# A global filter and a GELU layer on one core: half of one batch's input behind the batch before's read-back, table parts at other slots, and another spacing of the last batch

## The chip, the core and the metric

The kernel runs on one core of a Trainium2 chip. A core has a matrix engine (TensorE, PE in the profile; PEld is its loading of weights), three engines for vectors and scalars (VectorE or DVE, ScalarE or ACT, GpSimd or POOL), an engine that here only issues transfers (SyncE or SP), and 16 DMA engines that all transfers share. Each engine works through its own list of instructions in order and waits for the others by semaphores. The metric is the device time of one execution in microseconds (us); lower is better.

## What is computed

The input `x` has 8 batches of 3008 rows by 256 channels. The first half filters every channel of a batch along the rows by a product of Fourier transforms; the second half is a layer with exact GELU over all 24064 rows, with 2048 hidden columns:

```python
X = np.fft.rfft(x, axis=1)
Y = X * (filt_r + 1j * filt_i)[None, :, :]
y = np.fft.irfft(Y, n=3008, axis=1)            # 8 x 3008 x 256
h = y.reshape(24064, 256) @ w_in               # 256 x 2048
g = 0.5 * h * (1.0 + erf(h / sqrt(2)))
out = g @ w_out                                # 2048 x 256
```

## The kernel before

**The layer** runs over 47 tiles of 512 rows. A tile needs 16 calls of `mm1` (one 128-column piece of the hidden layer each: two matmuls into a bank of PSUM, then GELU on ScalarE into `g_sb`, L643). The second product (`mm2_seven`, L700) uses Strassen's scheme: seven products of quarters in place of eight. For it VectorE forms sums of quarters of `g_sb` (`sums_1`, L685; `sums_2`, L691; `sums_3`, L698), and combines the products in `t_sb` and `ost` (L731 to L745). `put_rows` stores finished rows from GpSimd's queue (L763). The buffers of `t_sb` and `ost` rotate through four places, three of which a tile uses, so tile 4's second `ost` (written from L739 on) reuses the place of tile 3's first, which is stored last of tile 3's.

**The filter** writes 3008 as 47 x 64 and does four small transforms per batch, with two trips through HBM to turn the data round:

- `load_next` (L148): GpSimd waits at a *gate*, a copy of one element of a given tile (`gate`, L143), and then issues the loads of a quarter of the next batch's input (`load_x_pairs`; two DMAs for half `h` = 0, four for `h` = 1). Four pieces `c`, two halves each. Both batches use one buffer.
- `fold` (L102) on VectorE, then `s1` (L415): matmuls, evacuation to `a_sb` by ScalarE and VectorE (L326, L328), written to an HBM scratch R1 from SyncE's queue.
- `r1` (L442) reads R1 into `b_sb`. For each of three units `u`: `s2` (L448) multiplies by a table, `s2_out` multiplies by the filter on VectorE (L468, four calls), `s2_sum` adds (L474, L475), `s3` (L477) transforms back, `s3_out` evacuates to `v_sb` on ScalarE and writes a scratch R2 (L498). The `s2` of the next unit uses the same four banks that the `s3` before it used.
- `r2` (L501) reads R2 back into `d_sb` (L506), in four pieces. `s4` (L509) makes 16 half units of a batch with the table `T4a` and evacuates them to `y_sb`, the input of `mm1`, on ScalarE (L326) or VectorE (L330).

Batch 0 goes through a form of its own ahead of the layer. The rest is interleaved with it.

**Order.** The order is written out by hand. A *slot* is one call of `mm1` (16 to a tile, 752 in all); `put(slot, f, ...)` hangs a call onto a slot, and what is emitted in a slot stands in each engine's list ahead of that slot's share of `mm2_seven` and its `mm1`. A slot number therefore sets an order and not a time. Tile 5 is special (`late`): it needs the first unit of batch 1, so slots 80 to 85 hold a double share of the second product and no `mm1`, and `s4` of batch 1's first two units stands at slots 82 to 85. `first(b)` is the first slot of the tile in which batch `b` begins; `s1`, `s2` and `s3` of a batch are set back from it by fixed numbers. A set of `busy` slots, made from these, moves the `s4` units to free slots, and `crowd` says which of them go to ScalarE.

**Tables.** `T4a`, the table of `s4`, is made on GpSimd in four parts of eight columns (`table_4_all`, L403): each part has four multiplies (L411) and two sums (L413). Units 2i and 2i + 1 of a batch read part i. Its scratch tile comes from the same three buffers as `d_sb`.

Of the kernel before, what the change touches and what calls it, by code (L numbers as in the profile page):

```python
# [31 lines left out]
class _Mix:  # L32
# [114 lines left out]

    def load_next(self, b, p, c, h):  # L148

        self.gate(self.st[b, "p", p][0:1, p % 2, 1, 0, 0:1])  # L150
        self.load_x_pairs(b + 1, c, h)

    def load_w_in(self):
# [631 lines left out]
def kernel(  # L785
# [9 lines left out]
    m = _Mix(ctx, tc, x, filt_r, filt_i, moe_w_in, moe_w_out, out)  # L795
    nc, B, S = tc.nc, m.B, m.S
# [116 lines left out]
    def put(slot, f, *a):  # L913
        at.setdefault(slot, []).append((f, a))

    def first(b):
        return (b * S // TCH) * 16

    busy, crowd, after = set(), set(), {}
    for b in range(1, B):  # L920
        hi = first(b)
        e = 4 * (b == B - 1)
        s1, n1, r1 = (4, 2.75, 16) if b == 1 else (hi - 87, 3.7, hi - 73) if b == 2 else (hi - 94 - e, 3.7, hi - 80 - e)
        s2 = (30, 43, 56) if b == 1 else (hi - 64 - 2 * e + (b == 2), hi - 48 - 3 * e + e // 4, hi - 32 - 3 * e)
        busy.update(range(s1 - 1, s1 + int(3 * n1) + 2))
        for c in range(4):
            slot = s1 + int(c * n1 + (b == 1 and c in (1, 2)))
            put((0, 1, 5, 8)[c] if b == 1 else (70, 74, 86, 94)[c] if b == 2 else hi - 94 - (20, 13, 8, 6)[c], m.fold, b, c)
            put(slot, m.s1, b, c)
        for u in range(3):  # L930
            put(r1 if u < 2 else s2[0] + 1, m.r1, b, u)
            put(s2[u], m.s2, b, u)
            for i in range(4):
                put(s2[u] + 2 * i + (b == 2 and u == 0), m.s2_out, b, u, i // 2, i % 2)
            for i in range(2):
                put(s2[u] + (9 + i if 1 < b < B - 1 else 7 + 2 * i), m.s2_sum, b, 2 * u + i)
            s3 = s2[u] + (13 if 1 < b < B - 1 else 11)
            put(s3, m.s3, b, u)
            put(s3 + 1, m.s3_out, b, u, 1)
            busy.update(range(s2[u] - 1, s2[u] + 5), range(s3 - 1, s3 + 2))  # L940
        after[b] = s3 + 4
        crowd.update(range(s2[0], after[b]), range(s1 + 66, s1 + 94))
        if b + 1 < B:
            for i, (u, o, p) in enumerate(((0, 5, 1), (0, 7, 1), (1, 1, 2), (1, 5, 3), (1, 7, 3), (2, 1, 4), (2, 5, 5), (2, 7, 5))):
                put(s2[u] + o, m.load_next, b, p, i // 2, i % 2)

    for b in range(1, B):
        end = 1000000
# [26 lines left out]
    put(14, m.table_4_factors, g)  # L975
    put(18, m.table_u)
    parts = [(w, h) for w in range(0, HB, 8) for h in range(2)]
    for i, slot in enumerate((15, 22, 45, 52)):
        put(slot, m.table_4_all, parts[2 * i:2 * i + 2])
    put(1, m.load_filters_again, nc.gpsimd, 0, 2)  # L980
    put(18, m.load_filters_again, nc.sync, 2, 4)
# [57 lines left out]
```

## Time and profile before

| | |
|---|---|
| median of 3 runs | 741.06 us (741.05 to 741.15) |
| the profiled execution | 740.78 us, span of the core 739.0 us |
| granted TensorE clock | 0.999 |
| busy: PE, DVE, ACT, POOL | 97%, 82%, 78%, 39% of the span |
| moved by DMA | 89.30 MB, mean 121 GB/s |

The span runs from the first to the last instruction. A row of the timeline gives start, length, engine, line, operation, output and inputs; in square brackets stands the time for which the engine had been idle and what ended that. "x7" is a row that merges seven like instructions. A row of the chain gives start, length and what the chain passed through. A row of the waits gives the total, how often, and the longest. Lengths of matmuls are modelled. Slots fall at these times: slot 22 ends at 56.7, slot 45 at 80.0, slot 52 at 86.0, slot 71 at 104.5, slot 79 at 110.9, slot 104 at 136.9 and slot 582 at 580.1 on TensorE; other engines may run ahead or behind.

### The profile page before, as it was taken

Reading aid. Unit: us, or ns where it says so; the run is one execution under the profiler, and the core shown is the slowest. Engines: PE = TensorE matmul, PEld = TensorE weight load, DVE = VectorE, ACT = ScalarE, POOL = GpSimd, SP = SyncE. Lnnn points to the kernel's source line nnn. Section 1 sums busy time; section 2 is a strip of 40 time slices with the busy share of each in tenths; the row PEclk is TensorE's granted clock in tenths of the full one; section 3 lists DMA queues with packets and bytes.
Section 4 is the critical chain, followed back from the end, with each engine's and each line's share of the span. In section 5 each row is a group of like instructions: output and inputs, shape, how many; then the busy total and the mean of one; then the engine's idle time right before and its main releaser. Section 6 shows DMA issues by size and latency. Waiting matters only on the chain.

```text
span 739.0 us, 22144 instructions
## 1 busy us (share of the span) xinstructions
PE 716.6 (97%) x9063; PEld 506.7 (69%) x9213; DVE 604.0 (82%) x1105; ACT 575.6 (78%) x1049; POOL 290.8 (39%) x547
## 2 busy tenths in 40 slices
PE   7998999999999999999999999999999999999998
PEld 4855665667777767676777667666667667777776
DVE  8987797899887998788986999779988898676566
ACT  6996677778887888778887788877888777777773
POOL 7898771346122653134611364115631122122121
PEclk9999999999999999999999999999999999999999
DMA  9996443755345643545535455345544433401011
GB/s 150 211 192 201 105 112 94 209 128 109 85 129 173 124 99 106 155 138 115 124 116 172 105 123 126 101 150 146 113 101 137 137 99 96 115 31 58 30 58 59
DMA packets 81190, 89.30 MB, mean 121 GB/s; under 512 B 13201, under 2 KB 60433, under 8 KB 81089
## 3 DMA queue, kind: packets, MB, share of 16 engines
q0 software_dynamic: 22480, 40.02, 23.5%
q1 hardware_dynamic: 58193, 47.66, 23.3%
q8 instruction: 72, 1.18, 0.7%
q14 instruction: 29, 0.24, 0.1%
q10 hardware_dynamic: 416, 0.20, 0.1%
HBM read 55.57 MB, written 48.23 MB: 140 GB/s over the span
## 4 chain that ended last, share of the span: by engine, by line
PE 87%; ACT 4%; DVE 3%; DMA 3%; issue 2%; POOL 0%; SPq 0%; another core or an unknown queue 0%; DVEq 0%; POOLq 0%; ACTq 0%
PE ps_o L716 38%; PE ps_h L640 37%; PE ps_s L515 3%; PE ps_s L430 2%; PE ps_o L656 2%; ACT g_sb L643 2%; PE ps_s L457 2%; PE ps_s L488 2%; DMA R<-v_sb 1%; ACT v_sb L326 1%; DVE p L468 1%; DMA d_sb<-R 1%; DMA x_sb<-in_x_dram 1%; PE ps_c L587 1%; ACT y_sb L326 1%
## 5 line engine op out<-in xcount | busy, mean ns | idle before, releaser
L643 ACT ACTIVATE g_sb<-ps_h 128x512 f16<-128x512 f32 x752 | 445.8, 603 | 141.1 <-PE ps_h L640 116.5
L640 PE MATMUL ps_h<-y_sb,w_in_sb 128*128 128x512 bf16 (+3 forms) x1454 | 414.4, 365 | 0.6
L763 POOL DMA_DIRECT2D out_dram<-ost x231 | 131.2, 575 | 398.5 <-DVE ost L745 390.0
L716 PEld LDWEIGHTS <-g_sb 128*128 128x128 f16 x2880 | 189.0, 98 | 84.5 <-issue 13.5
L716 PEld LDWEIGHTS <-s_sb 128*128 128x128 f16 x2160 | 145.0, 98 | 53.6 <-issue 3.7
L640 PEld LDWEIGHTS <-w_in_sb 128*128 128x128 bf16 x1600 | 125.7, 98 | 7.7 <-issue 1.3
L716 PE MATMUL ps_o<-w_sums,g_sb 128*128 128x128 f16 x1440 | 124.8, 220 | 2.4 <-DVE g_sb L691 1.0
L716 PE MATMUL ps_o<-w_sums,s_sb 128*128 128x128 f16 x1440 | 123.4, 219 | 1.7 <-DVE t_sb L731 0.2
L685 DVE TENSOR_TENSOR s_sb<-g_sb 128x1024 f16<-128x1024 f16 x180 | 119.5, 696 | 0.7 <-ACT g_sb L643 0.6
L716 PE MATMUL ps_o<-w_out_sb,g_sb 128*128 128x128 f16 x1440 | 116.5, 220 | 2.5 <-DVE ost L745 0.7
L468 DVE TENSOR_TENSOR p<-ps_s,F 128x1024 bf16<-128x1024 f32 x84 | 102.0, 1218 | 7.8 <-PE ps_s L457 6.2
L99 POOL DMA_DIRECT2D x_sb<-in_x_dram x156 | 79.0, 513 | 2.5 <-DMA x_sb<-in_x_dram 1.4
L716 PE MATMUL ps_o<-w_out_sb,s_sb 128*128 128x128 f16 x720 | 62.5, 219 | 0.9
L691 DVE TENSOR_TENSOR g_sb<-s_sb,g_sb 128x1024 f16<-128x1024 f16 x90 | 62.1, 691 | 1.5
L698 DVE TENSOR_TENSOR s_sb<-g_sb 128x1024 f16<-128x1024 f16 x90 | 61.5, 683 | 0.0
L738 DVE TENSOR_TENSOR t_sb<-t_sb,ps_o 128x256 f32<-128x256 f32 x45 | 18.8, 419 | 41.6 <-PE ps_o L716 41.1
L515 PEld LDWEIGHTS <-d_sb 96*128 96x128 bf16 x448 | 31.2, 97 | 28.6 <-DMA d_sb<-R 2.8
L326 ACT ACTIVATE y_sb<-ps_s 128x376 bf16<-128x376 f32 x95 | 45.5, 479 | 4.6 <-PE ps_s L515 4.6
L326 ACT ACTIVATE v_sb<-ps_s 128x512 bf16<-128x512 f32 x83 | 45.6, 610 | 1.6 <-PE ps_s L488 1.3
L745 DVE TENSOR_TENSOR ost<-t_sb,ps_o 128x256 f32<-128x256 f32 x88 | 32.9, 416 | 15.6 <-PE ps_o L716 15.6
L328 DVE CAST a_sb<-ps_s 128x512 bf16<-128x512 f32 x54 | 34.7, 684 | 11.6 <-PE ps_s L430 11.4
L733 DVE TENSOR_TENSOR ost<-t_sb,ps_o 128x256 f32<-128x256 f32 x45 | 18.7, 416 | 27.6 <-PE ps_o L716 27.6
(156 smaller groups left out, 565.4 us busy)
## 6 DMA issues: line engine op xcount, KB each, us to landing
out_dram<-ost POOLq DMA_DIRECT2D x127, 128.0 KB, 2.7
b_sb<-R SPq DMA_DIRECT2D x21, 512.0 KB, 5.0
R<-v_sb SPq DMA_DIRECT2D x84, 128.0 KB, 2.4
d_sb<-R SPq DMA_DIRECT2D x56, 192.0 KB, 3.8
R<-a_sb SPq DMA_DIRECT2D x108, 96.0 KB, 2.2
x_sb<-in_x_dram POOLq DMA_DIRECT2D x48, 94.0 KB, 2.7
x_sb<-in_x_dram POOLq DMA_DIRECT2D x48, 48.0 KB, 2.6
x_sb<-in_x_dram POOLq DMA_DIRECT2D x12, 188.0 KB, 5.1
```

What stands on the lines that cost most here:

```text
L99: self.nc.gpsimd.dma_start(out=xt[64 * v + to:64 * v + to + m, h, 4 * c:4 * c + 4 * n, :], in_=xv[h][at:at + m, w:w + 4 * n, :])
L326: self.nc.scalar.activation(out=out, in_=in_, func=AF.Copy, scale=1.0 if scale is None else scale)
L328: self.nc.vector.tensor_copy(out=out, in_=in_)
L468: v(out=w[:, a], in0=ps.unsqueeze(2).to_broadcast([128, 2, 2, 256]), in1=f.unsqueeze(1).to_broadcast([128, 2, 2, 256]), op=ALU.mult)
L515: nc.tensor.matmul(ps[:, 94 * i:94 * i + 94], lhsT=d[:, (grp % 2) * 4 + i, 128 * half:128 * half + 128], rhs=self.T4a[:, 4 * grp + i, 0:2 ...
L640: nc.tensor.matmul(ps[:, o:o + n], lhsT=w[:, dc], rhs=self.ring[:, dc, off:off + n], start=(dc == 0), stop=(dc == 1))
L643: nc.scalar.activation(out=self.st["g", t][:, jc, :], in_=ps, func=AF.Gelu)
L685: self.nc.vector.tensor_tensor(out=self.st["s", t][:, i:i + 2], in0=a, in1=b, op=ALU.subtract)
L691: self.nc.vector.tensor_tensor(out=a21[:, k], in0=self.st["s", t][:, k, 0], in1=a22[:, k], op=ALU.add)
L698: self.nc.vector.tensor_tensor(out=self.st["s4", t][:, k], in0=a12[:, k], in1=s2[:, k], op=ALU.subtract)
L716: nc.tensor.matmul(ps[:, (m + 1) % 2, sub, :], lhsT=a[:, i, 128 * sub:128 * sub + 128], rhs=b[:, i], start=i == 0, stop=i == 7)
L763: eng.dma_start(out=out, in_=tile_[lo - r0:lo - r0 + n])
```

## The change

```diff
@@ load_next
-        self.gate(self.st[b, "p", p][0:1, p % 2, 1, 0, 0:1])
+        if b == 1 and c > 1:
+            self.gate(self.st[b, "d", 0][0:1, 0, 0:1])
+        else:
+            self.gate(self.st[b, "p", p][0:1, p % 2, 1, 0, 0:1])
         self.load_x_pairs(b + 1, c, h)
@@ the order
-        s2 = (30, 43, 56) if b == 1 else (hi - 64 - 2 * e + (b == 2), hi - 48 - 3 * e + e // 4, hi - 32 - 3 * e)
+        s2 = (30, 43, 56) if b == 1 else (hi - 74, hi - 59, hi - 44) if e else (hi - 64 + (b == 2), hi - 48, hi - 32)
...
-            s3 = s2[u] + (13 if 1 < b < B - 1 else 11)
+            s3 = s2[u] + (11 if b == 1 else 12 if e or (b, u) in ((2, 0), (B - 2, 2)) else 13)
...
-                put(s2[u] + o, m.load_next, b, p, i // 2, i % 2)
+                put((76, 77, 80, 81)[i - 4] if b == 1 and i > 3 else s2[u] + o, m.load_next, b, p, i // 2, i % 2)
...
-    for i, slot in enumerate((15, 22, 45, 52)):
+    for i, slot in enumerate((15, 45, 52, 104)):
         put(slot, m.table_4_all, parts[2 * i:2 * i + 2])
```

It has three parts.

1. The second half of batch 2's input (pieces 2 and 3, loaded while batch 1 is in work) waits at its gates for the first piece of batch 1's read-back (`d_sb`, asked for at slot 71) in place of batch 1's products. Its four calls move from slots 50, 57, 61 and 63 to 76, 77, 80 and 81.
2. The four parts of `T4a` stand at slots 15, 45, 52 and 104 in place of 15, 22, 45 and 52.
3. In the last batch (batch 7) `s2` of unit 0 moves from slot 584 to 582, so that the units stand 15 slots apart (582, 597, 612), and `s3` follows `s2` after 12 slots in place of 11: slots 594, 609 and 624 for 595, 608 and 623. Its read-back moves from slot 627 to 628. Of the other batches, unit 0 of batch 2 and unit 2 of batch 6 have `s3` after 12 slots in place of 13 (125 for 126, and 540 for 541), and batch 6's read-back begins at slot 544 for 545.

Through `busy` some `s4` units move too: of batch 1, units 2 to 4 by a slot, and one half of unit 3 from slot 118 on ScalarE to slot 111 on VectorE; of batch 5, unit 7 from slots 537 and 539 to 538 and 542; of batch 6, one half of unit 3 from slot 582 on VectorE to slot 588 on ScalarE, and units 4 and 6 by a slot.

## The prediction

> **What bounds the kernel now.** I read the page first, then TensorE's waits, then the timeline around each wait and the chain of waits around the longest. All times are us from the span's start.
>
> ```profile
> PE 716.6 (97%) x9063; PEld 506.7 (69%) x9213; DVE 604.0 (82%) x1105; ACT 575.6 (78%) x1049; POOL 290.8 (39%) x547
> ...
> PE 87%; ACT 4%; DVE 3%; DMA 3%; issue 2%; POOL 0%; SPq 0%; another core or an unknown queue 0%; DVEq 0%; POOLq 0%; ACTq 0%
> ```
>
> TensorE is the bound: 97% busy, 87% of the chain that ended last. GpSimd is 0% of that chain, so moving its work pays only where it holds up somebody else. What can be won is TensorE's own idle time; TensorE's waits name it:
>
> ```profile
> PE ps_s L515 <- DMA d_sb<-R: 2.2, 2, 1.7
> ...
> PE ps_o L716 <- DVE g_sb L691: 1.0, 1, 1.0
> PE ps_s L488 <- DVE p L474: 0.9, 1, 0.9
> PE ps_s L457 <- ACT v_sb L326: 0.7, 3, 0.2
> PE ps_o L716 <- DVE ost L745: 0.7, 1, 0.7
> ```
>
> A wait costs a little more than its idle time. Seven 128-column matmuls take 0.55 and one is drawn 0.22 long, so they follow each other at 0.055 and 0.16 of a last one's length lies inside the wait; I add it. The timeline says where the L691 wait comes from:
>
> ```profile
> 66.52 1.31 POOL L413 TENSOR_TENSOR T4a<-tmp_sb 96x376 bf16<-96x376 f32 x1
> ...
> 66.92 1.46 DVE L685 TENSOR_TENSOR s_sb<-g_sb 128x1024 f16<-128x1024 f16 x1
> ...
> 68.42 0.69 DVE L691 TENSOR_TENSOR g_sb<-s_sb,g_sb 128x1024 f16<-128x1024 f16 x1
> ...
> 69.17 0.51 PE L716 MATMUL ps_o<-w_sums,g_sb 128*128 128x128 f16 x6 [0.99 <-DVE g_sb L691]
> ```
>
> That GpSimd operation belongs to the table part at slot 22. L685 usually takes 0.68; here, beside it, 1.46, and the L691 just before took 0.97 for 0.69. VectorE is busy without a break from 62.56 to 74, so TensorE receives this delay. The chain of waits for batch 1's read-back:
>
> ```profile
> 103.81 7.22 DMA R<-v_sb
> ...
> 111.47 3.08 DMA d_sb<-R
> ```
>
> and the timeline around it, with who was issuing at that time:
>
> ```profile
> 103.14 1.98 POOL L99 DMA_DIRECT2D x_sb<-in_x_dram  x4
> ...
> 111.79 2.82 POOL L763 DMA_DIRECT2D out_dram<-ost  x5 [4.90 <-DVE ost L745]
> ...
> 114.68 0.33 PE L515 MATMUL ps_s<-T4a,d_sb 96*128 96x94 bf16 x4 [1.65 <-DMA d_sb<-R]
> ```
>
> The last write of R needs 7.22 to land; page section 6 gives 2.4 as the median. It goes out amid ten loads of batch 2's input (99.61 to 105.1) and three stores. The remaining waits on TensorE, in its timeline:
>
> ```profile
> 159.51 0.41 PE L457 MATMUL ps_s<-b_sb,T2p 64*32 64x256 bf16 x15 [0.22 <-ACT v_sb L326]
> 551.73 0.33 PE L515 MATMUL ps_s<-T4a,d_sb 96*128 96x94 bf16 x4 [0.51 <-DMA d_sb<-R]
> 591.32 0.45 PE L716 MATMUL ps_o<-w_out_sb,g_sb 128*128 128x128 f16 x5 [0.66 <-DVE ost L745]
> 595.52 0.41 PE L457 MATMUL ps_s<-b_sb,T2p 64*32 64x256 bf16 x15 [0.22 <-ACT v_sb L326]
> ```
>
> **The table parts.** A part is four multiplies of 0.82 and two sums of 0.98: 5.3 alone, 6.1 as seen from 55.51 to 61.65. The one at slot 22 leaves 61.65 to 67.8 free. VectorE gets back 0.28 + 0.78 = 1.06, and of TensorE's 0.99 + 0.16 = 1.15 that much goes. Ends: 0 (another VectorE wait takes it) and 1.3 (0.18 at 70.63 goes too); I take 1.06, as that VectorE stretch has no idle time to swallow it. The wait of 0.88 at 74.15 stays: its VectorE and TensorE sides both move forward. The parts of slots 45 and 52 stay where parts already run. The one now at slot 104 runs behind five stores (129.59 to 132.4), so from 132.4 to 138.4; nothing but later stores queues behind it, the next at 143.66, and its readers (units 6 and 7) come from slot 153. Beside other parts VectorE lost 0.79 (two L685 in 2.07 for 1.28 at 58.79), 1.27 (L474 and L475 in 0.91 and 1.20 for 0.42 each, from 83.46) and 1.18 (at 94 to 97). VectorE idles 2.46 before 139.09, which covers that: cost 0, or up to 1.3 without this cover.
>
> The Trainium skill, "SBUF — State Buffer", section "Who interferes with whom", says that a VectorE instruction with two SBUF inputs and a GpSimd instruction that reads SBUF exclude each other for a whole instruction, the first one winning. That agrees with L685 here (it ended 0.55 after L413) and speaks against the part at slot 104: by it each of six operations could block one of VectorE's sums, an estimate of 5.3, less 2.46 idle, and the total below would be 738.3. The rows of the three other parts show at most 1.27, and I go by them.
>
> **Half of batch 2's input behind the read-back.** Four gates and twelve loads move from slots 50 to 63 to slots 76 to 81, in GpSimd's order now around tile 3's stores (slot 79). With none of them in flight, the last write (issued 103.81) lands after 2.34 (as unit 0's, issued at 77.89) to 3.75 (as batch 6's, beside stores, at 544.39): 106.2 to 107.6. SyncE then issues the reads, which land 3.1 to 3.5 later: 109.3 to 111.1. TensorE asks at 113.03, so the whole 1.65 + 0.16 = 1.81 goes. Ends 0 and 1.81.
>
> The added wait: GpSimd stands at the gate until about 109.3. Behind it are batch 2's loads and tile 3's stores, and VectorE waits for both. Two gates and six loads took 3.43 (101.68 to 105.11); the stores thus start at 112.8 instead of 111.79, the last is issued 2.27 later and lands 1.96 after that, 117.0. Its buffer is next written by tile 4's L739, at 118.92 before, 117.1 now: just in time. With the read-back at 110.8 VectorE would stall 1.4 there, and TensorE would lose 1.0 of it (the first cast of `s1` frees a bank 0.36 ahead of need). I take 0.1. The folds have slack: piece 2 issued by 112.8, landed about 115.5, folded at 117.8; piece 3 issued by 119.1, landed 121.8, folded at 125.1.
>
> **The spacings.** A whole `s2` undisturbed starts 0.56 before the next matmul (581.24 to 581.80); at 158.57 and 594.58 it takes 1.28, as ScalarE still empties `s3`'s banks. Both `s3` move one slot (0.82) earlier, and the second evacuation, ended at 159.46, would end by 158.64, before its bank is asked for at 158.84: 0.72 each. `s2_sum` is ready for it (VectorE done at 153.82, asked at 155.3). Batch 6's last `s3` and its read-back move one slot earlier: of 0.51 + 0.16 I take 0.6, since `s3` then meets `s2_sum` with no slack (539.66 against 539.7). In the last batch, `s2` two slots earlier starts VectorE's chain of multiplies at 579.95; its queue up to L745, 4 x 1.14 + 0.8 + 0.6 + 1.1 + 3 x 0.6 + 2 x 0.68 = 10.2, ends at 590.2, L745 at 590.9, while `s3`, now ahead, keeps TensorE until 591.2: 0.66 + 0.16 = 0.82 goes. The input for this earlier `s2` (second piece landed 578.34) is there. Ends 0 and each full wait. Units 2 to 4 of batch 1 and 3 of batch 6 shift by slots, two of them between ScalarE (0.48) and VectorE (0.46); ScalarE's idle 0.23 a slot covers it but for 0.1. Batch 7's later `s3` delay its read-back to about 632.1, asked for at 633.64: no cost.
>
> **Sum:** 1.06 + 1.81 - 0.1 + 2 x 0.72 + 0.6 + 0.82 - 0.1 = 5.53. The profiled execution took 740.78 (span 739.0): 735.25. The median of the runs is 0.28 higher: 735.5.
>
> **Rivals.** (a) Only part of it: a VectorE wait takes the first one's place (736.6), or the spacings in batches 2 and 7 give nothing because ScalarE, 78% busy, stays late (735.5 + 0.72 + 0.72 + 0.82 = 737.8); both together, 738.8. For it: VectorE is 82% busy, and these stretches have no idle time. (b) The write of R was not slow through the loads. Then the read-back lands at 114 as before, GpSimd starts the stores at 117.6, L739 stalls 3.0, TensorE loses 2.6: 5.53 - 1.71 - 2.6 = 1.2 gained, 739.9. Against it: beside stores alone a write took 3.75. (c) Slower: the jam moves with the loads. If the write still takes 5.05 (its neighbour's time) the read-back lands at 112.4; stores start at 115.9 and, landing in 6.3 like the one issued at 105.11, are done at 124.5. L739 stalls 7.4, TensorE loses 7.0 against 5.6 gained: 742.4, and 743.3 with 7.2 (the slowest load) for 6.3. It decides once tile 3's last store lands after 123.1. Against it: the R writes, half of the jam, are over by then. That the parts don't move at all, as slots only set the order, is excluded for slot 45: gates of earlier slots stand before it on GpSimd.
>
> **Chances.** Forecast 0.58 (own range 734.4 to 736.8), (a) 0.26, (b) 0.06, (c) 0.06, something between (a) and (b) 0.04. The range 734.4 to 738.3 takes the forecast, with every wait gone whole and half of the one at 74.15 at its lower end, and most of (a). A measurement of this kernel can tell about 0.2%, 1.5 us: faster is below 739.6. Faster 0.58 + 0.26 + 0.04 = 0.88; same 0.06 of (b) and 0.01 of (c); slower 0.05.
>
> **What would show it.** Right: no GpSimd sums between 61.7 and 70, L685 at 0.68 there, and no wait on L691; the last R write landing in under 4; no wait on `d_sb` before batch 1's first unit or batch 6's; `s2` at 0.56 in batches 2 and 7. Wrong: VectorE idle on a DMA before L739 or L107 near 117, TensorE then waiting on L328 or `ps_h`; L685 above 1 near 135 with TensorE waiting.

## The result and the profile after

The kernel after takes 737.09 us (median of 6 runs, 736.39 to 738.25), the kernel before beside it 741.05 (6 runs, 740.15 to 741.15): a ratio of 0.9951, interval 0.9938 to 0.9964, 3.96 us less. The forecast was 735.5. Its stated range, 734.4 to 738.3, holds the measured time; the narrower range that it gave for the forecast alone, 734.4 to 736.8, does not. The profiled execution took 737.13 with a span of 735.3, 3.65 less than the one before.

Line numbers: the new gate adds three lines, so from there on a line of the kernel after stands 3 higher than in the kernel before (L691 is L694, L716 is L719). Experiments without this gate keep the old numbers.

The page of after, busy time and the chain that ended last:

```profile
PE 716.1 (97%) x9063; PEld 506.5 (69%) x9213; DVE 604.6 (82%) x1105; ACT 575.4 (78%) x1049; POOL 291.2 (40%) x547
...
PE 88%; DVE 3%; DMA 3%; POOL 2%; issue 2%; ACT 1%; DVEq 0%; POOLq 0%
```

The same work on every engine, and still TensorE's chain. Of TensorE's waits in the layer, those on the lines that the forecast was about, each row with total, number and longest:

```profile
PE ps_o L719 <- DVE g_sb L694: 0.9, 2, 0.7
PE ps_s L491 <- DVE p L477: 0.9, 1, 0.9
...
PE ps_s L460 <- ACT v_sb L329: 0.2, 1, 0.2
```

The waits on `d_sb` and on `ost` are gone, those on `v_sb` are one for three. But the wait on VectorE's second sums is still there, 0.9 for 1.0, now twice. The timeline of after, first at the old place of the second table part, then around batch 1's read-back:

```profile
67.45 0.68 DVE L688 TENSOR_TENSOR s_sb<-g_sb 128x1024 f16<-128x1024 f16 x1
...
68.17 0.69 DVE L694 TENSOR_TENSOR g_sb<-s_sb,g_sb 128x1024 f16<-128x1024 f16 x1
...
101.65 2.55 SPq L501 DMA_DIRECT2D R<-v_sb  x4
...
106.03 1.22 SPq L509 DMA_DIRECT2D d_sb<-R  x2
...
108.75 0.47 POOL L146 COPY gate<-d_sb 1x1 bf16<-1x1 bf16 x1 [7.86 <-DMA d_sb<-R]
...
112.67 0.33 PE L518 MATMUL ps_s<-T4a,d_sb 96*128 96x94 bf16 x4
...
113.89 0.51 PE L719 MATMUL ps_o<-w_sums,g_sb 128*128 128x128 f16 x6 [0.21 <-DVE g_sb L694]
```

No sum lasts longer than 0.69 near 67, and no wait on L694 follows. The reads of R go out at 106.03, GpSimd stands at its gate until 108.75, and TensorE takes `d_sb` at 112.67 without a wait (no square bracket). Right behind it, at 113.89, it waits for L694. And at the new place of the last table part:

```profile
130.67 2.62 DVE L694 TENSOR_TENSOR g_sb<-s_sb,g_sb 128x1024 f16<-128x1024 f16 x1
...
131.11 1.61 POOL L414 TENSOR_TENSOR tmp_sb<-t_sb 96x376 f32<-96x376 f32 x2
...
132.81 1.32 POOL L416 TENSOR_TENSOR T4a<-tmp_sb 96x376 bf16<-96x376 f32 x1
...
133.34 0.51 PE L719 MATMUL ps_o<-w_sums,g_sb 128*128 128x128 f16 x6 [0.72 <-DVE g_sb L694]
```

L694 takes 2.62 where 0.68 is usual. It ends 0.57 after the second of GpSimd's multiplies, and TensorE waits 0.72 for it. The `s2` of batches 2 and 7 behind an `s3` (at 159.51 and 595.52 before) now run in one piece, with the next matmul 0.56 behind each start:

```profile
157.97 0.63 PE L460 MATMUL ps_s<-b_sb,T2p 64*32 64x256 bf16 x32
...
591.62 0.63 PE L460 MATMUL ps_s<-b_sb,T2p 64*32 64x256 bf16 x32
```

### A clock of slots

The medians of before in four comparisons lay between 740.06 and 741.05, and single runs between 739.4 and 742.4. So I read from every trace when TensorE begins the second of the two matmuls of a slot's `mm1`, and took the time between slots. The first column is that moment in slot 12, to which all kernels issue the same work. The stretches left out agree in all traces within 0.03 us (slot 130 to 500: 341.02 or 341.03; 602 to 745: 123.39 or 123.40).

| profiled execution | slot 12 at | 34 to 40 | 40 to 64 | 64 to 93 | 93 to 106 | 106 to 130 | 500 to 576 | 576 to 602 |
|---|---|---|---|---|---|---|---|---|
| before, first | 48.65 | 6.44 | 25.38 | **28.10** | 12.49 | 23.61 | 71.86 | 25.76 |
| b_again | 49.93 | 6.56 | 25.38 | 26.89 | 12.49 | 23.61 | 71.84 | 25.76 |
| b_look | 49.70 | 7.07 | 25.38 | 26.89 | 12.49 | 23.61 | 71.81 | 25.76 |
| e1_gates_only | 50.47 | 7.07 | 25.38 | 26.95 | 12.49 | 23.62 | 71.92 | 25.76 |
| e2_tables_only | 48.97 | 5.38 | 25.38 | 26.89 | 13.29 | 23.62 | 72.09 | 25.76 |
| e3_spacing_only | 49.58 | 7.08 | 25.38 | 26.90 | 12.49 | 22.77 | 71.18 | 24.08 |
| after, first | 49.46 | 5.37 | 25.38 | 26.96 | 13.38 | 22.77 | 71.18 | 24.08 |
| a_again | 49.82 | 5.38 | 25.38 | 26.94 | 13.38 | 22.78 | 71.18 | 24.08 |
| e4_part_at_86 | 50.85 | 5.38 | 25.38 | 27.36 | 12.43 | 22.77 | 71.18 | 24.08 |
| e7_old_parts | 49.92 | 6.44 | 25.38 | 26.97 | 12.46 | 22.78 | 71.18 | 24.08 |
| e5_slots_without_wait | 48.84 | 5.37 | 25.38 | 26.99 | 13.38 | 22.78 | 71.18 | 24.08 |
| e8_part_gated | 50.46 | 5.37 | 25.38 | 26.95 | 12.49 | 22.90 | 71.18 | 24.08 |
| e9_gated_part_old_loads | 49.78 | 5.37 | 25.38 | 26.90 | 12.49 | 22.86 | 71.18 | 24.08 |
| e10_sum_slot_38 | 50.10 | 5.38 | 24.60 | 26.99 | 12.49 | 22.95 | 71.18 | 24.08 |

### The profile page after: what moved, and what is told of

It is laid out like the page before. It is cut to its first block, busy times and chain, and to the rows that moved or that the text cites. A ratio compares the mean times of both kernels' runs of the same rounds, so it can differ in the third digit from the quotient of the medians.

```text
span 735.3 us, 22145 instructions
## 1 busy us (share of the span) xinstructions
PE 716.1 (97%) x9063; PEld 506.5 (69%) x9213; DVE 604.6 (82%) x1105; ACT 575.4 (78%) x1049; POOL 291.2 (40%) x547
## 4 chain that ended last, share of the span: by engine, by line
PE 88%; DVE 3%; DMA 3%; POOL 2%; issue 2%; ACT 1%; DVEq 0%; POOLq 0%
PE ps_o L719 40%; PE ps_h L643 38%; PE ps_s L518 3%; DMA x_sb<-in_x_dram 2%; PE ps_o L659 2%; PE ps_s L433 2%; PE ps_s L491 2%; PE ps_s L460 2%; DMA F<-in_filt_i_dram 1%; ACT g_sb L646 1%; DVE g_sb L694 1%; POOL F L141 1%; DVE s_sb L688 1%; DVE a_sb L331 1%; POOL x_sb L90 0%
## 5 line engine op out<-in xcount | busy, mean ns | idle before, releaser
L719 PEld LDWEIGHTS <-g_sb 128*128 128x128 f16 x2880 | 188.9, 98 | 84.4 <-issue 14.4
L719 PEld LDWEIGHTS <-s_sb 128*128 128x128 f16 x2160 | 145.3, 98 | 53.4 <-issue 3.1
L719 PE MATMUL ps_o<-w_sums,g_sb 128*128 128x128 f16 x1440 | 124.9, 219 | 2.4 <-DVE g_sb L694 0.9
L719 PE MATMUL ps_o<-w_sums,s_sb 128*128 128x128 f16 x1440 | 123.3, 219 | 1.9 <-DVE t_sb L734 0.2
L688 DVE TENSOR_TENSOR s_sb<-g_sb 128x1024 f16<-128x1024 f16 x180 | 119.2, 693 | 0.7 <-ACT g_sb L646 0.6
L719 PE MATMUL ps_o<-w_out_sb,g_sb 128*128 128x128 f16 x1440 | 116.4, 219 | 1.8
L694 DVE TENSOR_TENSOR g_sb<-s_sb,g_sb 128x1024 f16<-128x1024 f16 x90 | 63.7, 708 | 1.5
L719 PE MATMUL ps_o<-w_out_sb,s_sb 128*128 128x128 f16 x720 | 62.5, 219 | 0.9
```

What stands on the lines that cost most here:

```text
L688: self.nc.vector.tensor_tensor(out=self.st["s", t][:, i:i + 2], in0=a, in1=b, op=ALU.subtract)
L694: self.nc.vector.tensor_tensor(out=a21[:, k], in0=self.st["s", t][:, k, 0], in1=a22[:, k], op=ALU.add)
L719: nc.tensor.matmul(ps[:, (m + 1) % 2, sub, :], lhsT=a[:, i, 128 * sub:128 * sub + 128], rhs=b[:, i], start=i == 0, stop=i == 7)
```

## Experiments: each of the three parts alone

**The gates.** Before, with only the new wait and the new slots of batch 2's input:

```diff
+        if b == 1 and c > 1:
+            self.gate(self.st[b, "d", 0][0:1, 0, 0:1])
...
+                put((76, 77, 80, 81)[i - 4] if b == 1 and i > 3 else s2[u] + o, m.load_next, ...)
```

> The kernel before with the gates and their slots alone. Theory N (a new wait took over part of this step: the sums of tile 4 on VectorE, L691, end after TensorE asks for them near 113): the last write of R lands in under 4 us, the wait on d_sb before batch 1's first unit goes, a wait on L691 of 0.4 to 0.5 us stands just behind it, and the median is 1.0 to 1.3 us below before, about 739.9. Rival (the shortfall came from another part of the change, so that this part alone gives all of its 1.81): 739.2, with no wait on L691.

740.48 (11 runs, 739.81 to 742.18), before 740.65 (21 runs): ratio 1.0001, 0.9992 to 1.001. The last write of R lands in 2.3 us and TensorE does not wait for `d_sb`: what the gates are to do, they do. Yet the time is that of before, so neither theory's gain is there, and the wait on the second sums behind it is 0.21.

**The tables.** Before, with only the slots of the parts:

```diff
-    for i, slot in enumerate((15, 22, 45, 52)):
+    for i, slot in enumerate((15, 45, 52, 104)):
```

> The kernel before with the table parts at slots 15, 45, 52 and 104 alone. Theory N (the part at slot 104 holds an L691 of tile 5 for two of GpSimd's operations and TensorE waits for it): 1.06 us gained near 69, 0.9 lost near 133, an L691 above 2 us there, median 740.6 to 741.0. Rival, as predicted (VectorE's idle time covers the part): 740.0, no wait on L691.

740.5 (11 runs, 739.54 to 741.47): 0.9997, 0.9989 to 1.0006. The gain at slot 37 is there, and half of it or more is given back at slot 101, as the timeline of this kernel shows:

```profile
130.11 2.51 DVE L691 TENSOR_TENSOR g_sb<-s_sb,g_sb 128x1024 f16<-128x1024 f16 x1
...
130.45 1.62 POOL L411 TENSOR_TENSOR tmp_sb<-t_sb 96x376 f32<-96x376 f32 x2
...
132.68 0.51 PE L716 MATMUL ps_o<-w_sums,g_sb 128*128 128x128 f16 x6 [0.62 <-DVE g_sb L691]
```

Between slots 34 and 40 this kernel takes 1.06 to 1.69 less than the three executions of before. 0.80 is lost between slots 93 and 106, with the part as the only change there. What I had not expected: batch 2's loads stand as before, and still there is no wait on `d_sb`.

**The spacing.** Before, with only the new `s2` and `s3`:

```diff
-        s2 = ... (hi - 64 - 2 * e + (b == 2), hi - 48 - 3 * e + e // 4, hi - 32 - 3 * e)
+        s2 = ... (hi - 74, hi - 59, hi - 44) if e else (hi - 64 + (b == 2), hi - 48, hi - 32)
...
-            s3 = s2[u] + (13 if 1 < b < B - 1 else 11)
+            s3 = s2[u] + (11 if b == 1 else 12 if e or (b, u) in ((2, 0), (B - 2, 2)) else 13)
```

> The kernel before with the slots of s2 and s3 of part 3 alone. Theory: each wait goes whole as the trace of after shows, 0.73 near slot 128, 0.67 near slot 553 and 1.69 from slot 584 to 597, 3.1 us in all, median 738.0. Rival (the last batch's gain hangs on the earlier parts of the change): 738.8 to 739.7.

737.96 (5 runs, 736.32 to 738.21): 0.996, 0.9946 to 0.9973. By the clock 0.84 between slots 106 and 130, 0.68 between 500 and 576 and 1.68 between 576 and 602, 3.20 together. This is most of the change. Here too, the old loads bring no wait on `d_sb`.

## Experiments: is the slow write of R usual?

Two further profiled executions of before, unchanged.

> The kernel before, unchanged, for a second profiled execution. Theory V (the slow last write of R, 7.22 us in the first profiled execution, was an odd instance; it usually lands in 4.0 to 4.6 us beside the same loads, as with the tables alone and the spacing alone): the write lands in under 5 us and TensorE does not wait for d_sb near 114. Theory S (loads and write collide in every execution of before): 6 to 7.5 us again and a wait of 1 us or more on d_sb. Both: a wait of about 1 us on L691 near 69, and a ratio of 1.000 to the kernel before.

> The kernel before, unchanged, for a third profiled execution. Theory V: the last write of R lands in 4 to 5 us, no wait on d_sb near 114, and a wait on L691 of 0.2 or so at 115; between 0.5 and 1.1 lost at L691 near 70. Theory S: 6 us or more for the write and a wait of 1 us or more on d_sb.

741.06 (11 runs) and 741.2 (one run). The timeline of b_again, then of b_look:

```profile
103.24 2.56 SPq L498 DMA_DIRECT2D R<-v_sb  x4
...
109.79 0.84 SPq L506 DMA_DIRECT2D d_sb<-R  x2
...
114.27 0.33 PE L515 MATMUL ps_s<-T4a,d_sb 96*128 96x94 bf16 x4
...
115.48 0.51 PE L716 MATMUL ps_o<-w_sums,g_sb 128*128 128x128 f16 x6 [0.20 <-DVE g_sb L691]
```

```profile
68.60 1.46 DVE L685 TENSOR_TENSOR s_sb<-g_sb 128x1024 f16<-128x1024 f16 x1
...
70.85 0.51 PE L716 MATMUL ps_o<-w_sums,g_sb 128*128 128x128 f16 x6 [1.28 <-DVE g_sb L691]
...
103.51 2.55 SPq L498 DMA_DIRECT2D R<-v_sb  x4
...
111.15 0.84 SPq L506 DMA_DIRECT2D d_sb<-R  x2
...
114.56 0.33 PE L515 MATMUL ps_s<-T4a,d_sb 96*128 96x94 bf16 x4
```

The last write of R in the first execution of before, and then in that of e9_gated_part_old_loads (further below), which loads as before does:

```profile
101.84 2.57 SPq L498 DMA_DIRECT2D R<-v_sb  x4
...
111.09 0.84 SPq L506 DMA_DIRECT2D d_sb<-R  x2
```

```profile
101.91 2.57 SPq L498 DMA_DIRECT2D R<-v_sb  x4
...
108.28 0.84 SPq L506 DMA_DIRECT2D d_sb<-R  x2
```

In b_again and b_look, L515 follows without a wait. From the issue of the last write of R (the fourth of the merged row) to the issue of the reads, which wait for it, I find 7.28 in the first execution of before, but 4.58 and 5.67 in these, and 4.64, 4.48 and 4.40 in e2, e3 and e9, which load as before does. With the gates it is 2.40 to 2.59 (after, a_again, e1, e4, e7, e8, e10). So the loads do slow the write, by about 2 us and at most 3.3 in these five, but the read-back lands in time all the same (b_look lies between the two theories: a write longer than the 4 to 5 of V, and no wait); in b_look its first piece landed at 113.86 for a matmul at 114.56. Only the first profile lies beyond. The 1.2 us of the column "64 to 93" is its own. The order and spacing of this core's own transfers do not explain it: from 97 us on, e9 issues the stores, the loads and the writes in the same order, each 0.05 to 0.08 later, and its last write takes 4.40.

The other sign: the wait that the part at slot 22 causes is no constant. The stretch 34 to 40 takes 6.44 to 7.08 in the kernels with this part, 5.37 or 5.38 in all without it: 1.07 to 1.70 to be won.

**The order without the wait.** After, with its four calls at slots 76 to 81, but waiting for batch 1's products as before:

```diff
-        if b == 1 and c > 1:
-            self.gate(self.st[b, "d", 0][0:1, 0, 0:1])
-        else:
-            self.gate(self.st[b, "p", p][0:1, p % 2, 1, 0, 0:1])
+        self.gate(self.st[b, "p", p][0:1, p % 2, 1, 0, 0:1])
```

> The kernel after, with its four calls for batch 2's input at slots 76, 77, 80 and 81 but waiting for batch 1's products as before, which are long done there: the new order without the new wait. If the order does the work, the first two calls' loads are issued right behind tile 2's stores (near 100) and are over before the last write of R, which lands in 2.2 to 3 us; no wait on d_sb; the time is that of the kernel after, 737.1 to 737.5, within 0.5. If the wait is needed, the write takes 4 us or more, or TensorE waits for d_sb, with up to 1 us lost.

736.89 (6 runs, 736.64 to 738.19): 0.9949, 0.9934 to 0.9963, as after. The timeline of this kernel:

```profile
100.28 0.60 POOL L146 COPY gate<-p 1x1 bf16<-1x1 bf16 x1
...
100.82 1.12 POOL L99 DMA_DIRECT2D x_sb<-in_x_dram  x2
...
101.94 0.47 POOL L146 COPY gate<-p 1x1 bf16<-1x1 bf16 x1
...
102.35 1.99 POOL L99 DMA_DIRECT2D x_sb<-in_x_dram  x4
...
107.23 0.92 SPq L506 DMA_DIRECT2D d_sb<-R  x2
```

I was wrong about the order: GpSimd comes from tile 2's stores to these gates at 100.28, and six loads still go out amid the writes of R. The last write takes 4.21, and TensorE does not wait. The wait clears the queue and bought no time in this execution; that the six loads alone, with no store issued among the writes, slow the write is seen here too.

## Experiments: the part at slot 104

**A second look at after**, unchanged.

> The kernel after, unchanged, for a second profiled execution. Theory N (the last table part, at slot 104, makes VectorE's sum on L694 near 130.7 last through two operations of GpSimd in a row): L694 takes 2.4 to 2.7 us again and TensorE waits 0.6 to 0.8 for it. Rival (a chance meeting): L694 at 0.7 to 1.5 and no wait above 0.3. The last write of R lands in about 2.3 us. Time 736.4 to 738.3.

737.47 (5 runs, 736.66 to 738.03), before 740.06 (15 runs): 0.9963, 0.995 to 0.9975. L694 from 131.01 takes 2.61, GpSimd's two multiplies run from 131.44 for 1.61, TensorE waits 0.72: no chance meeting. In e5 the same sum takes 2.62.

**The part at slot 86 instead.** After, with one number changed:

```diff
-    for i, slot in enumerate((15, 45, 52, 104)):
+    for i, slot in enumerate((15, 45, 52, 86)):
```

> The changed kernel with the last table part at slot 86 in place of 104, so that GpSimd makes it right behind batch 2's loads (from about 119 to 125) instead of behind tile 4's stores (131 to 138). Theory N: L691 near 131 is back to 0.68, the wait of 0.9 near 133 goes, 0.9 us less than the changed kernel, 736.2, unless VectorE's folds and sums near 119 to 125 are held instead and TensorE with them. Rival (any part made while tiles are in work costs TensorE the same): 737.1, with the wait moved to between 119 and 127.

737.67 (5 runs, 736.87 to 737.98): 0.9958, 0.9946 to 0.9971. The wait near 133 is gone (0.95 less between slots 93 and 106), but the part hits a fold of batch 2 (L108 takes 1.37 for 0.69 in after), and the cast behind it ends late, in the timeline of this kernel:

```profile
120.29 2.68 POOL L414 TENSOR_TENSOR tmp_sb<-t_sb 96x376 f32<-96x376 f32 x2
120.31 1.37 DVE L108 TENSOR_TENSOR x_sb<-x_sb 111x1024 bf16<-111x1024 bf16 x1
...
122.94 1.02 PE L643 MATMUL ps_h<-y_sb,w_in_sb 128*128 128x512 bf16 x4 [0.27 <-DVE a_sb L331]
```

0.40 more between 64 and 93. The net 0.55 does not show in the medians; this kernel's profiled execution reached slot 12 1.39 later than that of after.

**The old parts.** After, with the parts back at slots 15, 22, 45 and 52 (the diff of the tables, reversed).

> The kernel after, with the table parts back at slots 15, 22, 45 and 52. If the parts act by VectorE's sums alone: the wait of 1 us near 70 comes back (1.07 lost), the one of 0.72 near 133 goes (0.90 gained), so 0.2 us longer than the kernel after, not told apart by the runs. If the whole 1.06 of the forecast was a gain and the part at slot 104 cost nothing, 1.06 longer: 738.1 or more.

737.75 (5 runs, 736.53 to 738.5): 0.9965, 0.9953 to 0.9978. By the clock 1.07 lost between 34 and 40 and 0.92 won between 93 and 106. So the move of the parts is worth 0.15 here, and up to 0.8 where the wait near 70 is at its longer value.

**The part a little later.** After, with a gate on the second piece of batch 1's read-back ahead of the last part:

```diff
+        if slot == 104:
+            put(slot, lambda: m.gate(m.st[1, "d", 1][0:1, 0, 0:1]))
         put(slot, m.table_4_all, parts[2 * i:2 * i + 2])
```

> The kernel after, with one more gate on GpSimd ahead of the last table part, on the last piece of a read-back that is long there (st[1, d, 1]), so that the part's order behind the stores of its slot is kept and its start is moved by little. Theory N: what counts is whether an operation of GpSimd runs while VectorE is at L694 ahead of TensorE's request; if the gate shifts the part past 132, L694 falls to 0.7 to 1.4 and TensorE gets up to 0.9 back (736.2 for 737.1); if it does not shift it, 2.4 to 2.7 and 737.1 as before. Rival (the part costs the same wherever it runs in this tile): 0.7 or more lost at another of VectorE's sums within 8 us, and 737.1.

736.62 (5 runs, 735.7 to 737.34): 0.9948, 0.9935 to 0.9962; a_again of the same comparison has 737.47. The timeline of this kernel:

```profile
131.65 0.69 DVE L694 TENSOR_TENSOR g_sb<-s_sb,g_sb 128x1024 f16<-128x1024 f16 x1
...
136.15 0.18 POOL L146 COPY gate<-d_sb 1x1 bf16<-1x1 bf16 x1 [4.08 <-DMA d_sb<-R]
...
136.29 1.60 POOL L414 TENSOR_TENSOR tmp_sb<-t_sb 96x376 f32<-96x376 f32 x2
...
138.69 0.42 DVE L741 TENSOR_TENSOR t_sb<-t_sb,ps_o 128x256 f32<-128x256 f32 x1 [2.46 <-PE ps_o L719]
...
140.27 2.31 DVE L688 TENSOR_TENSOR s_sb<-g_sb 128x1024 f16<-128x1024 f16 x2
```

Half of the part now lies in VectorE's idle 2.46. The other half lengthens two L688 from 1.28 to 2.31, for which TensorE does not wait; 0.89 comes back between 93 and 106, and 0.12 goes between 106 and 130. This is the forecast's cover, and it works once the part truly lies there.

## Experiments: a version that beats both

**Without the new gates on the input.** e8_part_gated, with `load_next` and its slots as before the change.

> e8_part_gated with batch 2's input loaded as before the change (slots 50 to 63, waiting for batch 1's products). Theory V (the new gates gain nothing in a usual execution, since the last write of R lands in 4.6 us beside the loads and d_sb is still in time): 736.6, within 0.5 of e8_part_gated, no wait on d_sb near 112. Theory S (the gates take 1 us or more off in most executions): 737.6 or more, and TensorE waits for d_sb there.

736.41 (6 runs, 735.92 to 738.14), before 740.9 (11 runs): 0.9942, 0.9928 to 0.9957. No wait on `d_sb`, and 26.90 between 64 and 93 for 26.95. The first part of the change can be left out.

**The wait on the products.** e8_part_gated, with one of VectorE's sums a slot earlier:

```diff
-                put(s2[u] + (9 + i if 1 < b < B - 1 else 7 + 2 * i), m.s2_sum, b, 2 * u + i)
+                put(s2[u] + (9 + i if 1 < b < B - 1 else 7 + i if b == 1 and u == 0 else 7 + 2 * i), m.s2_sum, ...)
```

> e8_part_gated with the second s2_sum of batch 1's unit 0 one slot earlier (38 for 39), ahead of tile 1's L736 and L739 on VectorE. If VectorE's order alone makes the wait of 0.87 on L477 near 74.9, the sums end 0.78 earlier, that wait falls to about 0.1, and the time to about 735.9. If ScalarE's evacuation or a bank that L736 and L739 free comes next, a wait of 0.4 or more shows behind it and little is gained.

735.45 (5 runs, 734.97 to 736.3): 0.9928, 0.9913 to 0.9942. Its slowest run is below the fastest of the 11 of after. In the timeline of e8, this wait stood behind two operations for which TensorE shows no wait there:

```profile
73.64 0.41 DVE L736 TENSOR_TENSOR ost<-t_sb,ps_o 128x256 f32<-128x256 f32 x1
...
74.08 0.42 DVE L739 TENSOR_TENSOR t_sb<-t_sb,ps_o 128x256 f32<-128x256 f32 x1
74.42 0.42 DVE L477 TENSOR_TENSOR p<-p 128x512 bf16<-128x512 bf16 x1
...
74.89 0.65 PE L491 MATMUL ps_s<-p,U 32*64 32x256 bf16 x16 [0.87 <-DVE p L477]
```

In that of e10 they have changed places, and `s3` runs through:

```profile
73.24 1.16 PE L491 MATMUL ps_s<-p,U 32*64 32x256 bf16 x32
73.28 0.42 DVE L477 TENSOR_TENSOR p<-p 128x512 bf16<-128x512 bf16 x1
...
73.95 0.41 DVE L736 TENSOR_TENSOR ost<-t_sb,ps_o 128x256 f32<-128x256 f32 x1
```

0.78 between slots 40 and 64, as the order of VectorE's operations gives it, and nothing came in its place.

## Why the forecast was right, and where it was not

The direction is right, and the gain is TensorE's idle time, as forecast; it was 3.96 (2.59 against the before and after of the second comparison) for 5.53. Of the two halves of the forecast one held: the three terms of the spacing, 2.76 of the 5.53, gave 3.15 to 3.20. The moved part and the gates, 2.77 together, gave 1.32 between the two first profiles, and only 0.2 to 0.8 against the other two executions of before. That 737.09 lies in the stated range is owed to its upper part, which was there for rival (a). It is luck too that the first profile of before had the slow write: its 1.14 stands in the 3.65 between the two profiles. Term by term, the two first profiles, and what the clock gives against the other executions of before:

| term | forecast | first profiles | against b_again, b_look |
|---|---|---|---|
| part leaves slot 22 | 1.06 | 1.07 | 1.19 to 1.70 |
| part arrives at slot 104 | 0 (bound 1.3) | -0.89 | -0.89 |
| `d_sb` in time, less the stall at tile 4 | 1.71 | 1.14 | -0.05 to -0.07 |
| `s3` of batch 2, moved units | 0.72 - 0.1 | 0.84 | 0.84 |
| batch 6's read-back | 0.6 | 0.68 | 0.63 to 0.66 |
| last batch | 1.54 | 1.68 | 1.68 |
| start-up, to slot 12 | 0 | -0.81 | +0.24 to +0.47 |

**Right:** the part's departure from slot 22 (1.06 against 1.07; as this wait varies, so close a match is luck), the shorter waits of the spacing, and the reason given for those of `s2`, that it waits for ScalarE to empty the banks: both `s2` run in 0.63 with no bracket, and the next matmul starts 0.56 after each, as forecast. The stall feared at tile 4's second `ost`, taken at 0.1, did not come: in after VectorE wrote it (L742) at 117.53 without a wait. The store that it was reckoned from was the wrong one: tile 3's last store landed only at 118.08, after this write. The semaphores for which L742 waits in the trace are those of tile 3's first three stores, landed by 116.14; so the buffer is not the one stored last, as the text ahead of the prediction has it.

**Failed: "VectorE idles 2.46 before 139.09, which covers that: cost 0".** The idle time exists, but it stands behind the operation that TensorE asks for. In the trace of before the five stores ended at 132.4, and an L691 ran from 132.06 to 132.75; so the part had to start on top of it:

```profile
129.59 2.79 POOL L763 DMA_DIRECT2D out_dram<-ost  x5 [14.98 <-DVE ost L745]
...
132.06 0.69 DVE L691 TENSOR_TENSOR g_sb<-s_sb,g_sb 128x1024 f16<-128x1024 f16 x1
```

I laid the part's 6 us against the idle time of the whole stretch instead of laying its first operation beside the row that ran at that moment. The bound of 1.3 held TensorE's cost, 0.89; the choice of 0 did not. VectorE lost 1.94 in this one sum, more than the 1.27 of a whole part by which the forecast went. The sign of being wrong, a sum above 1 near 135 with TensorE waiting, came at 130.67. e8 shows that this idle time does hide the part if it starts 5 us later.

On the same step, the Trainium skill, "SBUF — State Buffer", section "Who interferes with whom", has the order of issue decide which of two contending instructions blocks. The direction of its warning was right and its size, by my estimate 2.8 net, three times the 0.89 measured. By the starts of the rows the order would be the other one: L694 began 0.44, 0.43, 0.34 and 0.44 before GpSimd's multiply (after, a_again, e2, e5) and still ended 0.55 to 0.57 after the second multiply, while the two ran undelayed (1.61 or 1.62). Whether a row's start is the moment of issue, no run here shows.

**Failed: "so the whole 1.65 + 0.16 = 1.81 goes".** The mechanism, loads that slow the write of R, is shown (2.40 to 2.59 without them, 4.21 to 5.67 with them, 7.28 once). The size was taken from one execution, and the wait begins only beyond what the others reach. Even in this one, 1.14 came back and not 1.71: TensorE waits on the second sums close behind, 0.21 in the trace of after at 113.89. From the first `s4` (112.67) to the next, after takes 1.57; before took 0.95 (114.68 to 115.63). In the trace of before, VectorE was busy with an L691 pair until 114.03, which I had not set beside the 113.03 of TensorE's request. The rows, two of before and one of after:

```profile
112.74 1.29 DVE L691 TENSOR_TENSOR g_sb<-s_sb,g_sb 128x1024 f16<-128x1024 f16 x2
...
115.63 0.33 PE L515 MATMUL ps_s<-T4a,d_sb 96*128 96x94 bf16 x4
```

```profile
114.24 0.33 PE L518 MATMUL ps_s<-T4a,d_sb 96*128 96x94 bf16 x4
```

Of the missing 1.9 us, by the first profiles, the two steps make 0.89 and 0.57 and the start-up 0.81, against 0.44 that the spacing won beyond its forecast (0.22 in batch 2, 0.08 in batch 6, 0.14 in batch 7). The start-up is no effect of the change: its work is the same, and slot 12 begins anywhere from 48.65 to 50.85 in the 14 traces. Rival (a) had the right shape, a VectorE wait in place of the one removed, but looked for it in the old place; (b) is contradicted by the write of 2.4 behind the gates, and (c) by the same write and because tile 3's last store landed at 118.08 and not after 123.1.

What stays open: why the write of R took 7.28 in one execution of before, and how often it does; and by what order VectorE's sum and GpSimd's multiplies shut each other out.

## What to carry to other kernels

Idle time covers an added delay only if it lies between the delay and the operation that the bounding engine next asks for: lay the moved work's start beside the rows running at that moment. Before a wait on a transfer is counted as a gain, profile the same kernel a second and a third time; here 1.2 us belonged to one execution alone. Compare traces stretch by stretch, from one program point to another: it finds effects of 0.1 us that medians with a spread of 2 us hide.

## What was not expected of the hardware

- A VectorE sum with both inputs in SBUF, 0.68 alone, lasted 2.51 to 2.62 when two multiplies of GpSimd began just behind it (four traces), while the multiplies kept their 0.81 each.
- A write to HBM that lands in 2.4 us alone took 4.2 to 5.7 beside loads of GpSimd's queue (six traces), and 7.28 in one of three executions of before, though the transfers around it were issued in the order and at the distances of e9, which took 4.40.
- The start-up reached slot 12 at 48.65 to 50.85 us in 14 executions with the same work. Behind it, like stretches of the same order agreed within 0.3 us, apart from the slow write of R and the wait near 70.
